# A block-causal attention with a feed-forward layer: the first product by seven block products in seven pieces, the bound of v on ScalarE, and a new order

## The chip, the cores and the metric

The kernel runs on one core of a Trainium2 chip. The metric is the device time of one execution in microseconds (us); less is better. A profile is one execution taken by the hardware profiler. Its engines are named PE (TensorE, matrix products), PEld (TensorE's weight loads), DVE (VectorE), ACT (ScalarE), POOL (GpSimd) and SP (SyncE, which here issues nearly all transfers).

## What is computed

Attention over q, k, v of shape (8 batches, 8 heads, 576 tokens, 64), masked by blocks of 64 tokens, and behind it a layer of two matrix products with h * relu6(h + 3) / 6 between them, on 4608 tokens of width 512 with 2048 inner columns.

```python
scores = np.where(block_i >= block_j, q @ k.T / 8, -1e9)   # per head, blocks of 64
attn = softmax(scores); x = (attn @ v)                      # 4608 x 512 after regrouping
h = x @ w_in                                                # 512 x 2048
g = h * np.clip(h + 3.0, 0.0, 6.0) / 6.0
out = g @ w_out                                             # 2048 x 512
```

## The kernel before

**Precision.** Nearly every product is done on 16-bit halves: an operand is scaled, rounded to a high half, and what is left makes a low half; three products (high by high, high by low, low by high) are summed. The first token piece alone is done in 32 bits. Each matmul fills half of the array's columns (64 weights wide), and two of them, one for each half, stand side by side, so "a row" below is one such half matmul.

**Attention.** 32 slots (8 batches by 4 pairs of heads). For a slot `qk_prep` scales and splits q and k and a transposing DMA turns them, `s_group` makes scores, exponentials and their halves `ph` and `phl`, which transposing DMAs turn into `pT`, and `pv_group` multiplies with v and writes the token piece x. The scale of v is made once for a batch: `v_max` (L958) reduces each slot's tile `vnat` (128 x 640) to its largest magnitude on DVE, POOL takes the maximum over partitions, and the scale and its reciprocal follow.

**The layer.** The tokens are cut into 13 pieces (numbered 0 to 12) of 384 columns, the inner columns into 16 groups of 128 (or 8 pairs c). `ffn1_` (L1682) does an ordinary piece: per group 24 rows of 384 columns into the bank `h`. From piece SW = 7 on, `ffn1_seven` (L1581) takes its place: for each pair c it treats the 256 x 512 by 512 x 384 product as 2 x 2 blocks and does it by seven block products instead of eight (Strassen's scheme in Winograd's form): 84 rows of 192 columns into the banks `u` and `v`, with copies of partial sums (`kept`, or `ph` in the last pieces) and additions between them. Its weights' sums and differences are made once (`w_forms`, L1456) for all c, stored in DRAM (`dr_wf`), and loaded again for each piece and c (`w_get`, L1482): two loads of 256 KB, each into one of NWG = 4 buffers with the tag `wg`. `x_forms` (L1551) makes the sums and differences of the token piece. The second product has the like scheme from piece SG = 11 on; it isn't touched.

**Order.** Nothing is issued directly: a `Recorder` keeps every operation with its operands, and `schedule` (L463) then simulates the engines with a table of costs and takes, on each engine, the ready operation with the lowest key. A key is a planned time plus a number from the table SHIFT, by step (`f1 6 3` is piece 6, group 3 of the first product). All operations are emitted in `emit`, so every row of the profile has the line L673. Buffers with the tag `stage` are slots of one tile that the planner hands out; those with the tag `wg` are a pool's buffers.

Of the kernel before, what the change touches and what calls it, by code (L numbers as in the profile page):

```python
# [67 lines left out]
for _step, _by in (  # L68
# [38 lines left out]
    ("gw", (
        "0:10.7,1:7.9,2:15.4,3:22,4:0.9,6:-2.1,7:11,"
    )),
    ("load_next", (  # L110
        ":-2,"
    )),
    ("maxes", (
        "1:-4.9,2:4.6,3:-7.8,4:-4.4,8:-4.1,"
    )),
# [8 lines left out]
    ("pv_group32", (
        "0 0:0.2,0 1:2,1 0:-3.3,1 1:-2.3,1 2:-0.3,2 0:-3.7,2 1:3.1,2 2:7.1,3 0:-8.5,3 1:-1.3,3 2:15.8,"
    )),
# [1936 lines left out]
```

## Time and profile before

| what | value |
|---|---|
| time, median of 3 runs | 944.58 us (942.45 to 945.48) |
| the profiled execution's own time | 944.98 us |
| its span, first to last instruction | 943.2 us |
| PE, DVE, ACT busy | 99%, 93%, 79% |

The span is 1.78 us shorter than the execution that it was taken from. A busy PE is not yet a PE at its peak, because matmuls are pipelined and overlap in the records; so what a matmul costs is read here from where a run of them starts to where the next one starts. TensorE's granted clock is at the full 2.4 GHz level in every stretch shown below (the column PEclk).

### The profile page before, as it was taken

How to read it: one execution, taken by the hardware profiler on the slowest of the kernel's cores; microseconds unless marked ns; L12 is line 12 of the kernel's file. 1: busy time of each engine (PE TensorE's matmuls, PEld its weight loads, DVE VectorE, ACT ScalarE, POOL GpSimd, SP SyncE). 2: the span in 40 equal slices, each digit the busy share in tenths (PEclk: the TensorE clock that was granted, in tenths of full speed). 3: DMA queues.
4: the chain of work that ended last, by engine and by line, in shares of the span. 5: the costliest groups of instructions: out<-in, count | busy, mean ns of one | idle time of the engine just before them, and what ended most of it. 6: DMA issues, size and time to landing. Idle time of an engine off the chain costs nothing.

```text
span 943.2 us, 33175 instructions
## 1 busy us (share of the span) xinstructions
PE 933.3 (99%) x13478; PEld 704.6 (75%) x13478; DVE 876.6 (93%) x2293; ACT 749.4 (79%) x1995; POOL 43.0 (5%) x146
## 2 busy tenths in 40 slices
PE   8999999999999999999999999999999999999998
PEld 5666446878788776666666677888888888888997
DVE  7999999999889999999999899899898999899975
ACT  6988878888878888878887887888788888576753
POOL 3010100000000000000000000000000000000000
PEclk9999999999999999999999999999999999999999
DMA  7969878899879999988898899899798995442330
GB/s 192 264 215 253 205 137 174 159 185 163 153 158 154 185 166 186 202 159 164 161 192 171 160 221 161 158 208 198 171 210 171 204 199 133 106 124 70 103 92 35
DMA packets 430489, 158.53 MB, mean 168 GB/s; under 512 B 404992, under 2 KB 405504, under 8 KB 430336
## 3 DMA queue, kind: packets, MB, share of 16 engines
q1 hardware_dynamic: 429392, 156.09, 79.9%
q8 instruction: 105, 1.72, 0.8%
q14 instruction: 48, 0.39, 0.2%
q10 hardware_dynamic: 944, 0.33, 0.1%
HBM read 70.25 MB, written 13.63 MB: 89 GB/s over the span
## 4 chain that ended last, share of the span: by engine, by line
PE 87%; DVE 6%; ACT 3%; DMA 2%; issue 1%; POOL 0%; DVEq 0%; ACTq 0%; SPq 0%
PE o L673 36%; PE h L673 20%; PE v L673 9%; PE s L673 7%; PE u L673 6%; PE pv L673 6%; DVE st L673 1%; DVE stages L673 1%; PE sf L673 1%; DMA qkT<-qks 1%; PE pf L673 1%; DMA pT<-ph 1%; PE pt L673 1%; ACT stages L673 1%; DVE win L673 0%
## 5 line engine op out<-in xcount | busy, mean ns | idle before, releaser
L673 PE MATMUL o<-wout,g 128*64 128x512 f16 (+3 forms) x3234 | 409.2, 377 | 0.0
L673 PEld LDWEIGHTS <-g 128*64 128x64 f16 x3174 | 192.0, 110 | 80.6 <-DVE g L673 0.2
L673 PEld LDWEIGHTS <-win 128*64 128x64 f16 x4032 | 207.2, 110 | 46.5 <-issue 2.0
L673 PE MATMUL h<-x,win 128*64 128x384 f16 (+3 forms) x2474 | 220.0, 312 | 0.0
L673 ACT ACTIVATE p<-s,st,esc 128x64 f32<-128x64 f32 (+1 forms) x280 | 163.4, 587 | 12.3 <-DVE phl L673 6.8
L673 DVE TENSOR_REDUCE st<-s 128x1 f32<-128x64 f32 (+1 forms) x280 | 118.9, 444 | 1.9 <-PE s L673 1.6
L673 PEld LDWEIGHTS <-wg 128*64 128x64 f16 x2304 | 105.1, 110 | 8.5 <-issue 1.1
L673 DVE SCALAR_TENSOR_TENSOR g<-stages,g 128x384 f16<-128x384 f32 (+1 forms) x192 | 98.5, 516 | 9.9 <-ACT g L673 9.2
L673 ACT ACTIVATE g<-stages 128x384 f16<-128x384 f32 (+1 forms) x150 | 73.8, 492 | 37.8 <-DVE stages L673 30.0
L673 PE MATMUL s<-qkT 128*64 128x64 f16 (+7 forms) x1120 | 99.8, 287 | 0.0
L673 PEld LDWEIGHTS <-vhl 128*64 128x64 f16 x1680 | 72.8, 110 | 10.9 <-issue 2.4
L673 PEld LDWEIGHTS <-qkT 128*64 128x64 f16 x1120 | 59.3, 110 | 26.2 <-issue 5.8
L673 ACT ACTIVATE stages<-h,eg,sh 128x192 f32<-128x192 f32 (+1 forms) x112 | 62.8, 575 | 16.2 <-PE h L673 15.5
L673 PE MATMUL pv<-pT,vhl 128*64 128x192 f16 (+2 forms) x1680 | 73.8, 233 | 0.4 <-DMA pT<-ph 0.3
L673 PE MATMUL v<-x,wg 128*64 128x192 f16 x1152 | 67.1, 246 | 0.8 <-ACT kept L673 0.8
L673 DVE SCALAR_TENSOR_TENSOR ph<-p,st,ph 128x64 f16<-128x64 f32 (+2 forms) x168 | 67.0, 443 | 0.0
L673 DVE SCALAR_TENSOR_TENSOR phl<-p,st,phl 128x512 f16<-128x512 f32 (+1 forms) x84 | 64.2, 788 | 1.9 <-ACT phl L673 1.6
L673 DVE SCALAR_TENSOR_TENSOR stages<-stages,eg,h 128x384 f32<-128x384 f32 (+1 forms) x96 | 51.5, 538 | 5.7 <-ACT stages L673 5.2
L673 ACT ACTIVATION_READ_ACCUMULATOR p<-s,st,esc 128x1 f32 x280 | 55.3, 197 | 0.0
L673 ACT ACTIVATE ph<-p,st 128x64 f16<-128x64 f32 (+5 forms) x111 | 46.6, 462 | 9.0 <-DVE st L673 8.2
L673 ACT ACTIVATE st<-st,esc 128x1 f32<-128x1 f32 (+2 forms) x130 | 37.2, 290 | 17.1 <-DVE st L673 16.0
L673 ACT ACTIVATE stages<-u,eg,sh 128x384 f32<-128x384 f32 (+1 forms) x64 | 36.0, 588 | 15.1 <-DVE u L673 12.4
(206 smaller groups left out, 1458.9 us busy)
## 6 DMA issues: line engine op xcount, KB each, us to landing
wg<-dr_wf SPq DMA_DIRECT2D x96, 256.0 KB, 3.1
vnat<-in_v_dram SPq DMA_DIRECT2D x64, 128.0 KB, 3.0
qk<-in_q_dram SPq DMA_DIRECT2D x28, 288.0 KB, 3.4
qk<-in_k_dram SPq DMA_DIRECT2D x28, 288.0 KB, 4.1
out_dram<-stages SPq DMA_DIRECT2D x20, 256.0 KB, 3.0
rawi<-in_moe_w_in_dram SPq DMA_DIRECT2D x8, 512.0 KB, 4.4
rawo<-in_moe_w_out_dram SPq DMA_DIRECT2D x8, 512.0 KB, 4.5
dr_wf<-wf SPq DMA_DIRECT2D x16, 256.0 KB, 2.5
```

What stands on the lines that cost most here:

```text
L673: getattr(eng, method)(*map(self.place, args), **{k: self.place(a) for k, a in kw.items()})
```

## The change

Four edits, and with them a new table SHIFT.

1. SW goes from 7 to 6: piece 6 too is done by seven block products. So `pv_group` writes piece 6 as one 32-bit tile, `x_forms` runs for it, `w_get` loads 16 times more, and `w_forms` is planned earlier (WF0 from 4.5 to 3.9, its step from 0.2996 to 0.28).
2. For batches 1 to 7 `v_max` no longer takes the largest magnitude on DVE but the sum of squares on ACT (Square with an accumulator; the squares go to a tile `unread`). The root is taken roughly, by shifting the bits of the sum right by one: one more small DVE operation for a batch.
3. The buffers `wg` become slots of one tile that the planner hands out, as the stages are.
4. Two constants of 128 x 32 and some small tiles move into stage slots or share a tile.

```diff
-VM_ACT = 0
-SW, SA = 7, 11
+SW, SA = 6, 11
-WF0, WFD, WFL = 4.5, 0.2996, 9.7246
+WF0, WFD, WFL = 3.9, 0.28, 9.7246
...
-        "0 0:2,0 1:1.1,0 2:0.3,0 3:16.7,0 4:-1.5,0 5:0.4,0 6:0.1,0 7:-1.8,0 8:0.7,0 9:2.3,0 10:-0.5,"
+        "0 0:21.8,0 1:19,0 2:-10.3,0 3:-61.1,0 4:-94.4,0 5:-75.8,0 6:-46.8,0 7:-8.5,0 8:-1.6,0 9:-39,"
...
-        return str(getattr(a.tensor, "tag", "")).startswith("stage_")
+        return str(getattr(a.tensor, "tag", "")).startswith(("stage_", "wg_"))
...
+            low = 1.0
+            if nm[0] == "v" and nm != "v0":
+                nc.vector.tensor_scalar(pw.bitcast(I32), al.bitcast(I32), 1, None, op0=ALU.logical_shift_right)
+                al, low = pw, 2.0 ** -64
+            nc.vector.tensor_scalar(pw, al, TINY * low, 1.0 / (E_V * low), op0=ALU.max, op1=ALU.mult)
...
+        t, m = vnat[n % NVB], vmax[b][:, hp:hp + 1]
+        if b:
+            nc.scalar.activation(unread, t, AF.Square, accum_out=m)
         else:
-            absmax(vmax[b][:, hp:hp + 1], vnat[n % NVB], AX.XYZ)
+            absmax(m, t, AX.XYZ)
...
-        return attp.tile([P, 2, 2, 2 * P], F16, tag="wg", bufs=NWG, name=f"{nm}{c}_{i}")
+        return drp.tile([P, 2, 2, 2 * P], F16, tag="wg", bufs=NWG, name=f"{nm}{c}_{i}")
```

**ACT in piece 6.** Before, piece 6 asks ACT for `stages<-h6` (the first step of the activation) and the rounding `g6`, among work of the attention (`p`, `st`, `phl`, `ph`) and of the output of piece 5 (`osb5`, `o5`).

```order
L673 ACTIVATE stages_74<-h6_2_1388,eg_584,sh3_1_1217 128x384
L673 ACTIVATE osb5_1392<-o5_0_1258,so5_1391 128x512
L673 ACTIVATE st19_2_1479<-st19_2_1479,esc19_1383 128x2
L673 ACTIVATE g6_2_1390<-stages_74 128x384
L673 ACTIVATE p19_6_1484,st19_2_1479<-s19_2_1_0_1482,st19_2_1479,esc19_1383 128x448
L673 ACTIVATE osb5_1392<-o5_1_1259,so5_1391 128x512
```

After, at the same place:

```order
L676 ACTIVATE kept6_1396<-u6_2_1437 128x192
L676 ACTIVATE p19_7_1505,st19_2_1503<-s19_2_0_0_1504,st19_2_1503,esc19_1410 128x512
L676 ACTIVATE st20_1_1550<-st20_1_1550,esc20_1476 128x1
L676 ACTIVATE stages_74<-u6_2_1437,eg_585,sh3_4_1400 128x384
L676 ACTIVATE g6_4_1440<-stages_74 128x384
L676 ACTIVATE p19_6_1508,st19_2_1503<-s19_2_1_0_1506,st19_2_1503,esc19_1410 128x448
L676 ACTIVATE kept6_1396<-v6_3_1459 128x192
L676 ACTIVATE stages_74<-v6_2_1438,eg_585,sh3_4_1400 128x384
```

The copies `kept6` have come in between, and TensorE's next block product into the same half bank waits for them.

**SP in the middle of piece 6** (`qkT` and `pT` are the transposing DMAs of attention slots 19 to 21, `dr_wf` the stores of the weights' forms). Before:

```order
L673 DMA_TRANSPOSE qkT21_1510<-qks_92 128x27x128
L673 DMA_TRANSPOSE pT19_1_1478<-phl19_6_1486 128x8x128
L673 DMA qk22_1580<-in_q_dram 128x9x64
L673 DMA_TRANSPOSE pT19_1_1478<-phl19_7_1487 128x8x128
L673 DMA dr_wf6_0_1425<-wf6_0_1423 128x1024
L673 DMA qk22_1580<-in_k_dram 128x9x64
L673 DMA_TRANSPOSE pT19_1_1478<-phl19_8_1488 128x10x128
L673 DMA dr_wf6_1_1428<-wf6_1_1426 128x1024
```

After:

```order
L676 DMA wgs_75<-dr_wf3_1_1198 128x1024
L676 DMA wgs_75<-dr_wf6_0_1333 128x1024
L676 DMA_TRANSPOSE qkT21_1536<-qks_93 128x27x128
L676 DMA wgs_75<-dr_wf4_0_1250 128x1024
L676 DMA_TRANSPOSE pT19_1_1502<-phl19_6_1510 128x8x128
L676 DMA wgs_75<-dr_wf4_1_1253 128x1024
L676 DMA_TRANSPOSE pT19_1_1502<-phl19_8_1512 128x10x128
```

The loads of weight forms for piece 6 now stand among the transposes of slots 19 and 20; the stores of the forms that stood there have moved ahead.

**The bound of v for slot 12.** Before, on DVE:

```order
L673 TENSOR_REDUCE vmax3_810<-vnat0_104 128x1
L673 TENSOR_SCALAR st9_0_815<-st9_0_815,esc9_746 128x3
L673 TENSOR_SCALAR g2_4_789<-stages_74 128x384
L673 SCALAR_TENSOR_TENSOR g2_4_789<-stages_74,g2_4_789 128x384
L673 TENSOR_TENSOR st8_2_791<-st8_2_791 128x1
```

After, on ACT:

```order
L676 ACTIVATE ph0_91<-p8_2_763,st8_0_759 128x192
L676 ACTIVATE unread_108,vmax3_811<-vnat0_104 128x640
L676 ACTIVATE p8_3_782,st8_1_780<-s8_1_0_0_781,st8_1_780,esc8_721 128x256
L676 ACTIVATE p8_4_784,st8_1_780<-s8_1_1_0_783,st8_1_780,esc8_721 128x320
L676 ACTIVATE st8_1_780<-st8_1_780,esc8_721 128x1
```

The reduction has left DVE's queue, and one activation of 640 columns stands among ACT's exponentials.

## Rows read from the trace of the kernel before

**Rows 1.** The page: busy time of the engines over the span.

```profile
PE 933.3 (99%) x13478; PEld 704.6 (75%) x13478; DVE 876.6 (93%) x2293; ACT 749.4 (79%) x1995; POOL 43.0 (5%) x146
```

**Rows 2.** Stretches: from:to, length, each engine's busy us (instructions), PEclk, DMA share, GB/s.

```profile
0.00:50.00 50.00, 45.65 (x290) 30.43 (x291) 42.83 (x140) 40.17 (x120) 10.60 (x44) 1.00 0.85 227
...
300.00:540.00 240.00, 240.00 (x3177) 164.22 (x3172) 230.83 (x601) 198.97 (x534) 10.18 (x32) 1.00 0.90 172
540.00:660.00 120.00, 118.39 (x2013) 95.00 (x2009) 112.62 (x296) 98.63 (x277) 3.37 (x14) 1.00 0.98 190
660.00:780.00 120.00, 120.00 (x2089) 99.97 (x2086) 112.35 (x293) 100.73 (x275) 3.10 (x13) 1.00 0.94 190
780.00:940.00 160.00, 159.32 (x2942) 139.69 (x2938) 142.39 (x331) 102.78 (x239) 0.24 (x1) 1.00 0.34 91
...
540.00:570.00 30.00, 29.03 (x496) 21.75 (x491) 27.54 (x76) 23.27 (x63) 1.07 (x3) 1.00 1.09 210
```

**Rows 3.** The chain that ended last: start, us, what, rows in a run.

```profile
240.26 5.85 PE h L673 x72
...
691.29 0.50 PE v L673 x12
691.79 0.99 PE u L673 x24
```

**Rows 4.** Groups by form: line, engine, operation, shapes, count; busy, mean ns.

```profile
L673 PEld LDWEIGHTS <-win 128*64 128x64 f16 x4032 | 207.2, 110 | 46.5 <-issue 2.0 <-DVE stages L673 1.2
...
L673 DVE TENSOR_REDUCE vmax<-vnat 128x1 f32<-128x640 f32 x32 | 25.8, 808 | 0.2
...
L673 ACT ACTIVATE vhl<-vnat,rs_v 128x640 f16<-128x640 f32 x28 | 23.0, 821 | 0.1
...
L673 ACT ACTIVATE kept<-v 128x192 f32<-128x192 f32 x55 | 18.0, 328 | 5.1 <-PE v L673 4.9
L673 DVE TENSOR_TENSOR u<-u,kept 128x384 f32<-128x384 f32 x32 | 17.8, 557 | 6.7 <-PE u L673 5.7 <-ACT st L673 0.8 <-ACT kept L673 0.2
...
L673 DVE TENSOR_TENSOR v<-v,kept 128x192 f32<-128x192 f32 x32 | 11.4, 355 | 0.0
...
L673 ACT ACTIVATION_READ_ACCUMULATOR qks<-qk 128x1 f32 x56 | 10.9, 194 | 0.0
...
L673 DVE SCALAR_TENSOR_TENSOR x<-pv,x 128x192 f16<-128x192 f32 x20 | 6.6, 348 | 0.0
...
L673 DVE TENSOR_TENSOR stages<-x 128x384 f32<-128x384 f32 x12 | 6.5, 546 | 0.0
...
L673 DVE TENSOR_TENSOR xr<-x,xr 128x768 f16<-128x768 f32 x6 | 5.7, 944 | 0.0
```

**Rows 5.** Timeline at 559 to 571 us: start, us, what [idle before, releaser].

```profile
559.90 0.68 ACT L673 ACTIVATE qks<-qk 128x576 bf16<-128x576 f32 x1 [1.35 <-DMA qkT<-qks]
...
561.94 0.69 PE L673 MATMUL v<-xr,win 128*64 128x192 f16 x12 [0.40 <-DVE stages L673]
...
569.11 0.83 ACT L673 ACTIVATE phl<-p,st 128x640 f16<-128x640 f32 x1 [1.37 <-issue]
...
570.21 0.69 PE L673 MATMUL v<-x,wg 128*64 128x192 f16 x12 [0.78 <-ACT kept L673]
```

**Rows 6.** Tile wg: what its readers waited for, and its loads' time to landing.

```profile
  issue: 1.1, 1
...
DMA to landing us min/median/max: 2.5/3.1/5.4
```

**Rows 7.** SP's timeline at 764 us: a transpose and the weight load behind it.

```profile
764.09 5.15 SPq L673 DMA_TRANSPOSE qkT<-qks  x1
769.33 0.53 SPq L673 DMA_DIRECT2D wg<-dr_wf  x1
```

**Rows 8.** PE's timeline in the first microseconds, and at the end.

```profile
7.17 1.04 PE L673 MATMUL sf<-qkf 128*128 128x128 f32 x6 [1.17 <-DVE qkf L673]
...
932.77 6.67 PE L673 MATMUL o<-wout,g 128*64 128x512 f16 x60
```

More of the change, by code (lines that the diff above doesn't have):

```diff
@@ L69 @@
     ("f1", (
[16 rows of a table removed]
[16 rows of a table added]
     )),
     ("f2", (
[18 rows of a table removed]
[20 rows of a table added]
     )),
     ("gw", (
[L108 removed]
+        "0:3.6,1:-10.2,2:-30.3,3:-20,4:-44.3,5:14.4,6:0.6,7:7.3,"
     )),
     ("load_next", (
[L111 removed]
+        ":2.5,"
     )),
     ("maxes", (
[L114 removed]
+        "1:-8.6,2:4.9,3:25.7,4:2,8:2.7,"
     )),
     ("pv_group", (
[6 rows of a table removed]
[6 rows of a table added]
     )),
     ("pv_group32", (
[L125 removed]
+        "0 0:10.9,0 1:2.6,0 2:-8.8,1 0:-16.4,1 1:-0.5,1 2:32.4,2 0:-3,2 1:14.5,2 2:6.8,3 0:-3.4,"
@@ L126 @@
+        "3 1:-20.8,3 2:21.9,"
     )),
     ("qk_load", (
-        "4:-16.6,5:14.5,6:20,7:53.9,8:3,9:-7,10:30.3,11:26.4,12:1.6,13:45.8,14:4.6,15:-6.8,16:-6.6,"
-        "17:-3.2,18:3.5,19:-3.4,20:-12.4,21:-0.7,22:1.4,23:6.5,24:14.4,25:-20.6,26:2,27:0.4,28:63.8,"
-        "29:-15.9,30:-2.9,31:-0.5,"
+        "4:27.1,5:-5.4,6:-12.7,7:4.1,8:-12.6,9:28.2,10:-12.3,11:3.6,12:-14.3,13:29.5,14:9.8,15:9.3,"
+        "16:4.7,17:-6.5,18:-6.8,19:-36,20:-22.1,21:-32.7,22:-22.9,23:-1.3,24:0.8,25:23.4,26:42.9,"
@@ L131 @@
+        "27:-44.9,28:-22.3,29:-14.7,30:0.1,31:-5.8,"
     )),
     ("qk_load32", (
-        "0:-0.7,1:-9.7,2:-3,3:0.8,"
+        "0:-30.8,1:-39.5,2:-7,3:-1.8,"
     )),
     ("qk_load32_rest", (
-        "0:-1.9,1:-8.1,2:10.7,3:0.1,"
+        "0:-0.5,1:1.7,2:-15.1,3:4.3,"
     )),
     ("qk_prep", (
-        "4:0.2,5:-11.3,6:-10.5,7:0.7,8:-2.7,9:1.3,10:1,11:1.6,12:-4.7,14:2.8,15:2.4,16:5.5,17:-0.8,"
-        "18:13.3,19:18,20:17.7,21:0.8,22:-7.6,23:2.5,24:-4.7,25:-2.9,26:-0.5,27:-0.4,28:1,29:1.4,30:-1.1,"
@@ L141 @@
-        "31:-2,"
+        "4:-0.5,5:69.8,6:-32.1,7:3.1,8:5.7,9:7.7,10:-48,11:-0.4,12:8.7,13:-3.5,14:-8.7,15:-14.8,16:-16.3,"
+        "17:5.5,18:23.1,19:4.6,20:50.9,21:13.9,22:0.6,23:-43.3,24:-3.6,25:31.3,26:-10,27:-16.4,28:-32.3,"
+        "29:29,30:3.9,31:0.4,"
     )),
     ("qk_prep32", (
-        "0 0:5.8,0 1:-3.5,1 0:-6,1 1:7.1,2 0:35.5,2 1:1.1,3 0:-3.1,3 1:-0.3,"
+        "0 0:-13.2,0 1:55.8,1 0:1.5,1 1:7.9,2 0:52,2 1:-13.6,3 0:20.5,3 1:72.2,"
     )),
     ("s_block32", (
[4 rows of a table removed]
[4 rows of a table added]
     )),
     ("s_group", (
[9 rows of a table removed]
[9 rows of a table added]
@@ L179 @@
+        "13:5.8,14:-8.9,15:30.1,16:-25.9,17:29.4,18:-4.5,19:-10.9,20:10.6,21:-21.2,22:-26.8,23:-15.6,"
+        "24:-95,25:63.8,26:-62.1,27:30.1,28:-17.3,29:18.3,30:7.2,31:23.6,"
     )),
     ("v_max", (
-        "0:-21.7,1:-14.2,2:-19.1,3:3.3,4:3,5:-2.5,6:-0.9,7:-2.9,8:-3,9:4.9,10:19.5,11:2.3,12:5.7,13:22,"
-        "14:-11.9,15:-4,16:-5.5,17:-5.9,18:-1.7,19:5.7,20:-1.3,21:2.6,22:-8.6,23:13.6,24:-8.4,25:0.2,"
-        "26:-7.3,27:5.3,28:9.5,29:-15.8,30:-9.6,31:1.2,"
+        "0:-6.6,1:59.8,2:-7.1,3:-31.2,4:-25.3,5:3.2,6:-0.7,7:-1.5,8:-1.9,9:32,10:-14,11:11.3,12:-14.9,"
@@ L184 @@
+        "13:10.9,15:11.6,16:19.8,17:8.2,18:21,19:6.2,20:44.3,21:14,22:7.6,23:56.8,24:-10.3,25:-4.3,"
+        "26:-23.3,27:-103.6,28:3,29:-11.6,31:17.2,"
     )),
     ("v_prep", (
-        "4:2.5,5:9.7,6:3.4,7:17,8:-0.3,9:19.8,10:-19.7,11:-4.7,12:1.2,13:-1,14:-2.9,15:2.7,16:0.3,17:9,"
-        "18:-1.6,19:12.4,20:5,21:-0.1,22:1.7,23:0.7,24:-14.9,25:-0.4,26:-5.2,27:-10.8,28:-14.3,29:-3.7,"
-        "30:1.5,31:8,"
+        "4:-6.2,5:27.6,6:4.6,7:-10.5,8:-0.8,9:-4,10:-35.3,11:-0.8,12:5.5,13:43.4,14:3.9,15:10.6,16:24.2,"
@@ L189 @@
+        "17:-0.7,18:-5.6,19:-10.6,20:1.8,22:3.6,23:3.7,24:-39.8,25:86.6,26:-2.6,27:2.7,28:-4.5,29:25,"
+        "30:-11.6,"
     )),
     ("wf", (
-        "0:-3.6,1:-1,2:-0.6,3:3.7,4:-3.3,5:9.3,6:1.9,7:6.2,"
+        "0:33.2,1:-5.6,2:1.4,3:8.6,5:6.2,6:7.2,7:12.3,"
     )),
     ("wg", (
[5 rows of a table removed]
[6 rows of a table added]
     )),
     ("xf", (
-        "7:-3,8:1,9:0.8,10:-1.3,11:10,12:-2.1,"
+        "6:2.6,7:-28.2,8:1.6,9:33.7,10:-6.7,11:-3.4,12:22.2,"
     )),
@@ L665, in schedule @@
         self.span = max(o.end for o in ops)
-        self.slot = {x: f[1] for x, f in got.items() if self.meta[x][0].startswith("stage_")}
+        self.slot = {x: f[1] for x, f in got.items() if self.meta[x][0].startswith(("stage_", "wg_"))}
         return sorted(ops, key=lambda o: (o.start, o.n))
@@ L678, in place @@
             return a
-        base = self.stages if a.dtype == F32 else self.stages.bitcast(a.dtype)
+        base, slots = self.rings[str(a.tensor.tag).split("_")[0]]
+        base = base if a.dtype == F32 else base.bitcast(a.dtype)
         (pitch, n), *dims = a.ap
@@ L682, in place @@
         row = base.ap[0][0]
-        return bass.AP(base.tensor, p0 * row + self.slot[a.tensor.name] * (row // self.NST) + f0, [(row, n), *dims])
+        return bass.AP(base.tensor, p0 * row + self.slot[a.tensor.name] * (row // slots) + f0, [(row, n), *dims])
 @with_exitstack
@@ L720 @@
     T0 = TP
-    nc.NST = NST_B
     NTA, NTR = 3, 2
@@ L741 @@
     drp = ctx.enter_context(tc.tile_pool(name="dr", bufs=1, space=bass.MemoryType.DRAM))
-    nc.stages = wpool.tile([P, NST_B * DM], F32, tag="stages", name="stages")
+    nc.rings = {x: (wpool.tile([P, n * DM], F32, tag=x + "s", name=x + "s"), n) for x, n in (("stage", NST_B), ("wg", NWG))}
     ps_s = ctx.enter_context(tc.tile_pool(name="ps_s", bufs=3, space=bass.MemoryType.PSUM))
@@ L799 @@
     ident = wpool.tile([P, P], F32, tag="ident", name="ident")
-    ramp = wpool.tile([P, 32], F32, tag="ramp", name="ramp")
-    rows = wpool.tile([P, 32], F32, tag="rows", name="rows")
+    ramp, rows = (drp.tile([P, 32], F32, tag="stage", bufs=4, name=x) for x in ("ramp", "rows"))
     nc.gpsimd.memset(ident, 0.0)
@@ L817 @@
         nc.gpsimd.memset(halves[h * BLK:(h + 1) * BLK, h * BLK:(h + 1) * BLK], 1.0)
-    one = wpool.tile([P, 1], F32, tag="one", name="one")
+    few = wpool.tile([P, 2], F32, tag="few", name="few")
+    one, three = few[:, :1], few[:, 1:]
     nc.gpsimd.memset(one, 1.0)
-    three = wpool.tile([P, 1], F32, tag="three", name="three")
     nc.gpsimd.memset(three, 3.0)
@@ L939 @@
         nc.gpsimd.memset(t[BLK:, NJ - 1], 0.0)
+    unread = wpool.tile([P, NJ, 2, D], BF16, tag="unread", name="unread")
     vscale = {}
@@ L959, in v_max @@
         b, hp = divmod(n, NPAIR)
-        if n < VM_ACT:
-            ab = attp.tile([P, S], F32, tag="p", bufs=NPB, name=f"va{n}").bitcast(BF16)
-            ab = ab[:, :NJ * 2 * D].rearrange("p (j h d) -> p j h d", h=2, d=D)
-            nc.scalar.activation(ab, vnat[n % NVB], AF.Abs, accum_out=vmax[b][:, hp:hp + 1])
+        t, m = vnat[n % NVB], vmax[b][:, hp:hp + 1]
+        if b:
+            nc.scalar.activation(unread, t, AF.Square, accum_out=m)
         else:
-            absmax(vmax[b][:, hp:hp + 1], vnat[n % NVB], AX.XYZ)
+            absmax(m, t, AX.XYZ)
         if hp == NPAIR - 1:
@@ L1086, in qk_prep32 @@
                 ]
-                parts = [parts[0][:, :S], parts[1], attp.tile([P, 4 * P], F32, tag="wg", bufs=NWG, name=f"qkf{n}_2")]
+                parts = [parts[0][:, :S], parts[1], drp.tile([P, 4 * P], F32, tag="wg", bufs=NWG, name=f"qkf{n}_2")]
             qkT[n] = parts[0], []
@@ L1157, in s_block32 @@
         if i % 2:
-            pr = attp.tile([P, 4 * P], F32, tag="wg", bufs=NWG, name=f"pf{n}_{i}")
+            pr = drp.tile([P, 4 * P], F32, tag="wg", bufs=NWG, name=f"pf{n}_{i}")
         else:
@@ L1670, in ffn1_f32 @@
             )
-        r = attp.tile([P, T0], F32, tag="wg", bufs=NWG, name=f"r0_{f}")
+        r = drp.tile([P, T0], F32, tag="wg", bufs=NWG, name=f"r0_{f}")
         nc.scalar.activation(r, ps, AF.Relu, bias=three, scale=1.0)
```

9 lines of the change are left out of this document (3 added, 6 removed), and 125 rows, old and new, of the table SHIFT.

## The prediction, as put on record

> **What bounds the kernel now.** I began with the page's engine totals: PE is busy for 99% of the span, DVE for 93%, ACT for 79% [rows 1]. A busy PE may still hide waits, so next come the stretches [rows 2]. PE misses 4.35 us of the first 50 us (50 less 45.65), none at all of the 240 us from 300 to 540, 1.61 us from 540 to 660, none from 660 to 780 and 0.68 us of the last 160. Over those stretches that is 6.6 us of idleness, so nearly all of the time is PE at work. The third view is the chain that ended last, to see whether the work itself runs at its pace: 72 rows of `h` take 5.85 us from start to start, 81.25 ns each, and 24 rows of `u` take 0.99 us, 41.25 ns each [rows 3]. Half as many columns take half the time, plus next to nothing. So in mid-kernel the price of an edit is the number of rows that it takes from PE or gives it, and everything else counts only where it makes PE wait.
>
> **The change part by part.**
>
> *Piece 6 by seven products.* Removed: 16 groups of 24 rows of 384 columns, 384 rows by 81.25 ns = 31.20 us. Added: 8 pairs c of 84 rows of 192 columns, 672 rows by 41.25 ns = 27.72 us. Both stand on PE, which waits for nothing in the stretch where piece 6 lies now, so the difference is on the path: **-3.48 us**. No other matmul changes in number.
>
> The Trainium skill, in "TensorE: Matmul & The Clock Gate", section "LDWEIGHTS (loading the stationary operand)", speaks against this: it prices a weight load by its columns divided by 1.2 in ns, 53 ns for 64 columns. If the loads of two rows side by side had to be done one after the other and set the pace, a pair would need 107 ns, an estimate by which the 336 new pairs would cost 35.9 us and the sum would be +4.7 us. The runs of 41.25 ns a row, load included, don't show that pace [rows 3].
>
> *What piece 6 then asks of DVE and ACT.* DVE gets 8 additions into `u` (557 ns), 8 into `v` (355), and in `x_forms` 8 operations of 384 columns (546), one of 768 (944) and one more of 546; it loses 8 lower halves of x (348) [rows 4]: 4.46 + 2.84 + 4.37 + 1.49 - 2.78 = +10.4 us. The 24 copies `kept` at 328 ns are 7.9 us on ACT or DVE, and the six roundings of `x_forms`, priced as their subtractions, 3.7 us. None of it is on PE; what hides it is the free time of the two engines. From 300 to 540 they are busy for 230.83 + 198.97 of 480 us [rows 2], so 50 us are free, and the 22 us asked for fit, the more as `w_forms`, whose operations stay the same in number, moves ahead of piece 6. If that cover were gone, PE would wait for a copy or for a rounded `g`, by about 0.4 to 0.8 us at a time, as it does at 561.94 and 570.21 [rows 5].
>
> *The bound of v on ACT.* DVE loses 28 reductions of 808 ns, 22.6 us. ACT gets 28 activations of 640 columns. A Square with an accumulator isn't in the trace; the nearest rows are the scaling of the same tile, 821 ns, and the reading of an accumulator, 194 ns [rows 4]. So 1.0 us each, 28.4 us in all, at the least 0.8 and at the most 1.1 us. Behind each stand exponentials and copies on ACT's queue, as the order shows, and a late `kept` can reach PE. It is one such delay for each attention slot, and ACT is free for 4.8 to 5.1 us in 30 (240 - 198.97 = 41 in 240, 120 - 100.73 = 19.3 in 120) [rows 2]. Cost: nothing on PE, down to -0.5 us (DVE earlier) and up to +1 us. The small shift for each batch is seven DVE operations, far off the path.
>
> *Loads and the queue of SP.* 16 more loads of 256 KB stand among the transposes. From 300 to 540 the DMA share is 0.90, with the loads from 540 to 660 it is 0.98, and 1.09 in its first 30 us [rows 2]. In those 30 us PE loses 0.97 us, and its two waits trace back to ACT waiting for a transpose that was late: 1.35 us for `qkT`, and 1.37 us in front of a `phl` whose buffer a transpose still read (the profile names no engine, so this is an inference) [rows 5]. From 660 to 780 the same loads run at 0.94 and PE loses nothing. Piece 6 takes some 75 us of the kernel. At the pace of 540 to 660 that is 1.0 us, at the pace of 660 to 780 it is 0. I take the middle: **+0.5 us**, and keep 0 and 1.0.
>
> *The slots of `wg` and the new order.* How long a weight load may take is given by the work on PE between the last reader of its slot and its first reader. Counted in rows, that work is under 9 us for 33 of 92 loads before and for 61 of 108 now; the shortest is 5.5 us before and 5.9 now. A load lands after 3.1 us, 5.4 at worst [rows 6], and a `qkT` transpose ahead of it can hold SP for 5.15 us [rows 7]. Before, all the short ones together cost PE one wait of 1.1 us that may be theirs [rows 6]. I take 0 and keep +1. The start and the end have no reason to change by much: 4.35 us of waiting in the first 50 us, the first of it for the copies of the first transposed q and k, which stand in the same order as before [rows 8]; behind them scores, exponentials and transposes of the first slots stand in another order, and that may give or take 2 us. At the end the same 60 rows of `o` close the program [rows 8]. Taken: 0.
>
> **The sum.** -3.48 + 0.5 = **-3.0 us**. The profiled execution took 944.98 us, so 942.0; it lies 0.4 us over the median of the runs, so the median becomes **941.6 us**. Its own bounds: -3.48 to -3.48 + 1.0 + 1.0, with -0.5 for DVE: 940.6 to 943.1, about 940.3 to 943.2 with the runs' scatter.
>
> **The rivals.**
>
> *The new order also takes out waits.* For it: PE idles 1.61 us from 540 to 660 and 4.35 us at the start, and a new order moves both. Against: the start is a chain of dependent steps. If the first goes and a quarter of the second (1.1 us): 944.58 - 3.48 - 2.7 = 938.4 us.
>
> *The start gets longer.* If its waits grow by half (2.2 us): 944.58 - 3.0 + 2.2 = 943.8; if they double, 945.9.
>
> *The transposes come late all through pieces 6 to 10: slower.* Place: ACT waits for `qkT` or `pT`, and behind it on its queue stand the copies `kept` that PE needs. For it: just that happened at 560 and 570, DVE and ACT together get 28 us more work (-22.6 + 28.4 + 22), and the room for loads is smaller. Against: 660 to 780 is free of it at the same load. Price: 0.97 us for each 30 us, as in the stretch from 540 to 570, over the 11 such stretches from 450 to 780 is 10.7 us, less the 1.6 that are there now, so 944.58 - 3.48 + 9.1 = 950.2 us. It decides the sign where it passes 3.48 us, and the bound of slower below from 6.3 us, 0.7 us for each 30.
>
> *The weight loads don't hide.* 288 rows more bring 288 more loads of 110 ns [rows 4]; if all were exposed, 31.7 us, and if one in four, 7.9 us: 944.58 - 3.48 + 7.9 = 949.0. The pace in rows 3 speaks against it.
>
> **How the numbers follow.** The runs lie within 0.3%, and a difference under 0.3% (2.8 us: 941.75 to 947.4) can't be told from none. The forecast 0.42, of which a little over half (0.24) is under 941.75. The order takes out waits: 0.23, all faster. The start longer: 0.13 (0.10 same, 0.03 slower). Late transposes: 0.20 (0.07 same, 0.13 slower). Exposed loads: 0.02, slower. So faster 0.47, same 0.35, slower 0.18. The range goes from 937.5, which leaves out the best fifth of the second case, to 949.0, which leaves out the worse half of late transposes: 0.15 in all.
>
> **What would show it.** The row counts of `u`, `v` and `h`, and a run of `u` rows at 41.25 ns also where piece 6 lies. PE's idleness in 30 us steps from 450 to 540: under 1 us in all if I am right, 1 us in each if the transposes come late, with ACT waiting for DMA `qkT` or with "issue" in front of `phl`. PE busy in the first 50 us beside 45.65. DVE's total lower by some 10 us and ACT's higher by 30 to 40 if the copies go to ACT. I am wrong in the main if piece 6 runs at 41 ns and the time still doesn't fall; then the order has turned the gain into waits elsewhere, and the stretches will show where.

## The result, and the profile after

| | median, us | lowest to highest | runs |
|---|---|---|---|
| before | 943.77 | 942.45 to 945.48 | 6 |
| after | 951.81 | 949.08 to 952.01 | 6 |
| forecast | 941.6 | range 937.5 to 949.0 | |

The changed kernel takes 1.0076 times as long (95%: 1.006 to 1.0093): slower by 8.0 us, where 3.0 us less were forecast. Its profiled execution took 949.68 us, with a span of 947.9 us. It is one of the two shorter of the six, and the profiled execution of the kernel before (944.98 us) lies above its median: so the two traces are 4.7 us apart where the medians are 8.0.

The page of the kernel after, totals of the engines (compare [rows 1]):

```profile
PE 933.3 (98%) x13764; PEld 713.2 (75%) x13764; DVE 877.1 (93%) x2324; ACT 767.9 (81%) x2051; POOL 41.9 (4%) x144
```

Its stretches, in the columns of [rows 2]:

```profile
0.00:50.00 50.00, 46.03 (x292) 30.77 (x293) 43.83 (x142) 40.36 (x124) 10.48 (x42) 1.00 0.84 221
50.00:300.00 250.00, 247.14 (x2933) 172.97 (x2933) 230.40 (x637) 211.21 (x552) 14.84 (x42) 1.00 0.92 181
300.00:540.00 240.00, 239.58 (x3474) 179.14 (x3472) 232.40 (x612) 203.85 (x558) 8.78 (x31) 1.00 0.95 184
450.00:540.00 90.00, 90.00 (x1476) 72.75 (x1473) 84.61 (x222) 76.32 (x207) 3.16 (x12) 1.00 1.02 200
540.00:660.00 120.00, 120.00 (x2083) 95.80 (x2080) 114.71 (x309) 105.63 (x292) 3.06 (x13) 1.00 1.07 197
660.00:780.00 120.00, 117.44 (x1992) 91.47 (x1987) 110.02 (x289) 103.35 (x288) 4.56 (x15) 1.00 0.97 190
780.00:940.00 160.00, 159.17 (x2978) 140.81 (x2976) 143.87 (x339) 102.99 (x240) 0.15 (x1) 1.00 0.37 94
```

The products of piece 6 lie between about 463 and 532 us, and there PE waits for nothing. The loss is elsewhere. PE idles 2.86 us from 50 to 300, where it idled 0.10 before, and 2.56 us from 660 to 780, where it idled not at all. The 1.61 us from 540 to 660 are gone, and the start is no longer than it was (3.97 us for 4.35).

The span grew by 4.7 us although PE has 3.5 us less to do, so 8.2 us of waiting were added. The idleness in the stretches shows 3.9 of it (10.64 less 6.74 us): a matmul's recorded duration stretches over part of a wait. Measured from start to start against the pace of each kind of row, behind the first 60 us, the excess is 3.5 us before and 11.9 after, and it sits at some twenty places: mainly 126, 171 to 201, 225, 300, 420, 684 to 711 and 727 to 783 us.

What the engines waited for there is seen best at the tile `phl`. Before, its writers waited once for a transposing DMA that still read the buffer, and twice with no releaser named, as at 569.11 [rows 5] (releaser, us in total, times):

```profile
  issue: 1.9, 2
...
  DMA pT<-phl: 0.6, 1
```

After, nine times for the DMA:

```profile
  DMA pT<-phl: 6.6, 9
```

One of the nine, in the timeline of the kernel after:

```profile
219.95 1.41 DVE L676 SCALAR_TENSOR_TENSOR phl<-p,st,phl 128x512 f16<-128x512 f32 x2
...
222.07 2.68 SPq L676 DMA_TRANSPOSE pT<-phl  x2
...
227.06 0.83 ACT L676 ACTIVATE phl<-p,st 128x640 f16<-128x640 f32 x1 [1.75 <-DMA pT<-phl]
...
227.79 0.47 ACT L676 ACTIVATE x<-pv 128x384 f16<-128x384 f32 x1
227.92 0.88 DVE L676 SCALAR_TENSOR_TENSOR phl<-p,st,phl 128x640 f16<-128x640 f32 x1 [1.70 <-ACT phl L676]
...
228.72 0.55 DVE L676 SCALAR_TENSOR_TENSOR x<-pv,x 128x384 f16<-128x384 f32 x1
...
229.33 0.46 PE L676 MATMUL s<-qkT 128*64 128x320 f16 x4 [1.49 <-DVE x L676]
```

A slot has three `phl` tiles and the pool has two buffers for them. At 222.07 SP issues the transposes of the first two; ACT must write the third into the first's buffer and waits 1.75 us until that transpose has read it. Behind this instruction on ACT's queue stands the copy `x<-pv`, behind it on DVE's the second half of that copy, and PE's next matmul waits for that: 1.49 us. In the kernel before, the same place goes without a wait, though its third tile follows its transposes by only 4.2 us:

```profile
219.12 2.74 SPq L673 DMA_TRANSPOSE pT<-phl  x2
...
223.35 0.82 ACT L673 ACTIVATE phl<-p,st 128x640 f16<-128x640 f32 x1
```

The transposes also land later than before. From 150 to 300 us the median from issue to landing of those into `pT` is 4.4 us, and it was 3.8, though the traffic is nearly the same (171 GB/s for 169). Why they land later isn't shown.

### The profile page after: what moved, and what is told of

Read it like the earlier page. It is cut to its first block, busy times and chain, and to the rows that moved or that the text cites. A ratio compares the mean times of both kernels' runs of the same rounds, so it can differ in the third digit from the quotient of the medians.

```text
span 947.9 us, 33891 instructions
## 1 busy us (share of the span) xinstructions
PE 933.3 (98%) x13764; PEld 713.2 (75%) x13764; DVE 877.1 (93%) x2324; ACT 767.9 (81%) x2051; POOL 41.9 (4%) x144
## 4 chain that ended last, share of the span: by engine, by line
PE 71%; DVE 14%; ACT 6%; DMA 5%; issue 2%; SPq 1%; POOL 0%; ACTq 0%; DVEq 0%
PE o L676 30%; PE h L676 12%; PE v L676 10%; PE u L676 7%; PE s L676 5%; PE pv L676 5%; DMA pT<-phl 3%; DVE st L676 2%; DVE phl L676 2%; DVE stages L676 2%; ACT p L676 2%; DVE ph L676 2%; ACT stages L676 2%; DVE g L676 1%; DVE wout L676 1%
## 5 line engine op out<-in xcount | busy, mean ns | idle before, releaser
L676 PE MATMUL h<-x,win 128*64 128x384 f16 (+3 forms) x2098 | 186.7, 311 | 0.2
L676 ACT ACTIVATE p<-s,st,esc 128x384 f32<-128x384 f32 (+2 forms) x280 | 163.1, 587 | 14.3 <-DVE phl L676 6.5
L676 PEld LDWEIGHTS <-wgs 128*64 128x64 f16 x2688 | 122.5, 110 | 11.6 <-issue 1.0
L676 DVE TENSOR_REDUCE st<-s 128x1 f32<-128x384 f32 (+6 forms) x280 | 119.1, 446 | 2.0 <-PE s L676 1.7
L676 PE MATMUL s<-qkT 128*64 128x512 f16 (+7 forms) x1120 | 102.2, 287 | 4.1 <-ACT p L676 2.5
L676 PE MATMUL v<-x,wgs 128*64 128x192 f16 x1344 | 77.9, 246 | 0.5 <-ACT kept L676 0.5
L676 DVE SCALAR_TENSOR_TENSOR ph<-p,st,ph 128x64 f16<-128x64 f32 (+3 forms) x168 | 67.8, 445 | 0.6 <-ACT ph L676 0.5
L676 ACT ACTIVATE stages<-h,eg,sh 128x192 f32<-128x192 f32 (+1 forms) x96 | 52.4, 560 | 9.8 <-PE h L676 7.2
L676 ACT ACTIVATE ph<-p,st 128x256 f16<-128x256 f32 (+5 forms) x116 | 48.7, 462 | 6.9 <-DVE st L676 5.8
L676 ACT ACTIVATE stages<-v,eg,sh 128x384 f32<-128x384 f32 (+1 forms) x72 | 41.8, 596 | 8.4 <-PE v L676 4.3
```

Source lines behind the costliest of these rows:

```text
L676: getattr(eng, method)(*map(self.place, args), **{k: self.place(a) for k, a in kw.items()})
```

## The experiments

Four theories: **V**, the bound of v costs ACT more than was allowed; **T**, the added weight loads crowd the transposes; **O**, the new order itself has the waits in it; and **B**, formed after the first runs, that late transposes act through the two buffers of `phl`. A new table of times would give a wholly different order, so all runs keep the order of their kernel (but for those that move instructions on purpose) and change an operation where it is emitted. Differences below are to the median of the kernel before in the same batch, that is, of the runs made together (943.17 to 944.11 us), by which the kernel after stands at +8.0 us.

### The bound of v

**e1_v_on_dve**, the kernel after:

```diff
+if method == "activation" and args[2] == AF.Square:
+    self.nc.vector.tensor_reduce(
+        self.place(kw["accum_out"]), args[1], axis=AX.XYZ, op=ALU.max, apply_absolute_value=True
+    )
+    continue
```

> The changed kernel with its order held, instruction by instruction; only the bound of v for batches 1 to 7 is again a largest magnitude on DVE (28 reductions at the places where the 28 activations stood). The changed kernel takes 951.8 us, the kernel before 943.8. Theory V (the bound on ACT holds up ACT): the 8 us come back for the larger part, 946 us or less. Theory T (weight loads crowd the transposes): no change beyond the one wait that the trace shows behind an activation `unread` (ACT waits 1.24 us for vnat at 300 us, PE loses 0.9 us there), so 950.5 to 952. Theory O (the waits are in the new order itself): the same 950.5 to 952, or a little more, since DVE gets 22.6 us of work that the order has no room made for.

Measured: 964.75 us, +21.6.

**e3_v_on_act**, the kernel before:

```diff
+if method == "tensor_reduce" and args[0].tensor.name[:4] == "vmax" and args[0].tensor.name != "vmax0":
+    self.nc.scalar.activation(self.nc.unread, args[1], AF.Square, accum_out=args[0])
+    continue
```

> The kernel before with its order held; only the bound of v for batches 1 to 7 is made as in the change, 28 Squares with an accumulator on ACT at the places of the 28 reductions, and one small DVE shift for a batch. Theory V: slower by most of the 8 us, 948 us or more. Theories T and O: 28 activations of about 0.92 us fit where ACT was free, 943 to 946 us.

Measured: 953.36 us, +10.2. Of this, about 2 us are lost at the start: the condition didn't catch batch 0, whose bound the kernel after leaves on DVE (32 Squares in the trace, not 28). So at a held order the work has no room on either engine that wasn't planned for it. Neither number is the price of the edit itself; for that the work was shortened where it stands.

**e5_short_square**, the kernel after, and **e8_before_short_max**, the kernel before:

```diff
+if method == "activation" and args[2] == AF.Square:
+    args = (args[0][:, :1, :1], args[1][:, :1, :1], AF.Square)
```

```diff
+if method == "tensor_reduce" and args[0].tensor.name[:4] == "vmax":
+    args = args[0], args[1][:, :1, :1]
```

> The changed kernel with its order held; only the 28 Squares on ACT read 64 of their 640 columns, so v is scaled by a bound from a tenth of the numbers. That takes some 0.65 us from each, 18 us from ACT. Theory V (the bound of v on ACT is what makes the changed kernel late): the larger part of the 8 us comes back, 946 us or less. Theory T (weight loads crowd the transposes): only the stall of 0.9 us at 300 us may go, 950.5 to 952. Theory O (the new order leaves too little between a result and its reader, on all engines): ACT is less often late, 949.5 to 951.

> The kernel before with its order held; only the 32 reductions for the bound of v on DVE read 64 of 640 columns, which takes some 0.7 us from each, 22 us from DVE: the gain that the change can have from DVE at most. Theory V and T: DVE's free time is cover enough, 943 to 944 us. Theory O: a little of the 3.5 us of stalls goes, 941.5 to 943 us.

Measured: 950.00 us, +5.9, so 2.1 us less than the kernel after; and 942.18 us, -1.9, with DVE busy for 860.9 us where it was 876.6. These edits shorten the work and don't remove it: a Square with its accumulator from 0.92 to 0.44 us, a reduction from 0.81 to 0.21. What they took away was worth about as much on ACT as on DVE, so moving the bound shows no gain. The 0.92 us of a whole Square are near the 1.0 that was taken:

```profile
L676 ACT ACTIVATE unread<-vnat x28: 719/727/762, 74.2 to 705.2; 128x640 bf16<-128x640 f32 x28
L676 ACT ACTIVATION_READ_ACCUMULATOR unread<-vnat x28: 185/192/226, 74.8 to 705.8; 128x1 f32 x28
```

(Tile `unread` of the kernel after: count, least, median and greatest ns, first and last start.) What was missed is that ACT's time isn't free.

### The weight loads

**e2_half_loads**:

```diff
+if method == "dma_start" and str(getattr(args[0].tensor, "tag", "")) == "wg" and args[0].dtype == F16:
+    args = args[0][:, :512], args[1][:, :512]
```

> The changed kernel with its order held; only each of the 112 loads of weight forms brings 128 KB in place of 256 KB (the first 512 of 1024 columns), so the other half of those operands holds older numbers and the output is not the reference's. PE does the same matmuls. Theory T (weight loads crowd the transposes): the stalls that end in a late transfer go, 1.6 us at 225, 0.9 at 300, 2.2 from 699 to 711 and perhaps 1.2 at 783 to 813 us, so 946 to 947 us. Theory V: 951 to 952. Theory O: only a part of these goes, 949 to 951, since the order leaves some readers too close behind their transfer even at light traffic, and the stalls at 126, 684, 735 and 759 us have no transfer at their end.

Measured: 952.03 us, but the edit had no effect: the tiles don't carry that tag at this point, and the loads in its trace still have 256 KB. It stands as a second measurement of the kernel after, +8.9, and shows that figures from single batches are good to about 1 us. Its trace is of an execution of 951.91 us, and there a `phl` that waited only 0.33 us in the trace of the kernel after (at 295.57 us) waits 2.69 us and holds PE up for 2.15:

```profile
296.93 0.72 ACT L678 ACTIVATE phl<-p,st 128x512 f16<-128x512 f32 x1 [2.69 <-DMA pT<-phl]
...
299.16 0.52 PE L678 MATMUL s<-qkT 128*64 128x384 f16 x4 [2.15 <-ACT p L678]
```

So in one and the same kernel it differs between executions which of these places costs time.

**e6_half_loads**, the kernel after, and **e7_before_half_loads**, the same edit in the kernel before:

```diff
+if method == "dma_start" and args[0].tensor.name[:2] == "wg" and args[0].dtype == F16:
+    args = args[0][:, :512], args[1][:, :512]
+if method == "matmul" and args[1].tensor.name[:2] == "wg" and args[1].dtype == F16:
+    w = args[1]
+    args = args[0], bass.AP(w.tensor, w.offset - w.offset % 1024 + w.offset % 512, w.ap), args[2]
```

> The changed kernel with its order held; each of the 112 loads of weight forms brings 128 KB in place of 256 KB, and the matmuls take all their weights from the half that was loaded, so the output is not the reference's. (In the earlier run e2_half_loads the edit did not reach the loads: they still brought 256 KB, so that run is a second measurement of the changed kernel, 952.0 us.) Theory T: the stalls that end in a late transfer go, 946 to 947.5 us. Theory V: 951 to 952. Theory O: 949 to 951, since the transposes are late by their own order and by each other.

> The kernel before with its order held and the same edit: its 96 loads of weight forms bring 128 KB each. Theory T: the stalls around 560 and 570 us go, 942 to 942.5 us. Theories V and O: 942.5 to 944 us; what this edit gives here is to be taken from what it gives to the changed kernel.

Measured: 947.57 us, +3.5, and 942.72 us, -1.4. Half the bytes give 4.6 us in the kernel after and 1.4 in the kernel before: the kernel after, with 112 such loads for 96, depends more on the transfers' pace. **e10_both_short** has the edits of e5 and e6 together:

> The changed kernel with its order held and two edits at once: Squares over 64 columns (alone -1.8 us, 950.0) and weight loads of 128 KB (alone -4.2 us, 947.6). The output is not the reference's, since half of the weight forms is left out. If V and T are separate parts of the loss they add up, 945 to 946.5 us, and the 4 us that then remain over the forecast of 941.6 are the order's. If they relieve the same stalls, 947 to 948 us.

Measured: 948.48 us, +4.8, no better than the half loads alone.

**e14_no_loads_for_6**, the kernel after without the 16 loads that piece 6 added (its products read `win` instead), and **e16_before_no_loads_for_7**, its counterpart for the first such piece of the kernel before:

```diff
+if method == "dma_start" and args[0].tensor.name[:4] == "wg6_":
+    continue
+if method == "matmul" and args[1].tensor.name[:4] == "wg6_":
+    args = args[0], self.nc.win[:, 0, 0, 0, :64], args[2]
```

> The changed kernel with its order held; the 16 weight loads that piece 6 adds are left out, and the matmuls of piece 6 that used them take weights from the tile `win` (so piece 6 is not the reference's). PE, DVE and ACT do the same work; SP issues 16 transfers less. Theory T, by count: the traffic is that of the kernel before, and of the 2.8 us that halving all loads gave here more than in the kernel before, most comes back: 948 to 949.5 us. If only the loads of the last pieces, behind which the larger stalls stand (684 to 814 us), matter: 951 to 952, since piece 6 (450 to 525 us) shows no stall. My prediction had +0.5 us for these loads: 951.3.

> The kernel before with its order held and without the 16 weight loads of its first piece by seven products, piece 7 (the same edit; its numbers are not the reference's): the control for e14_no_loads_for_6. Its stalls at 560 and 570 us stand right there, so 942 to 943.5 us; what it gives is to be taken from what e14_no_loads_for_6 gives.

Measured: 950.46 us, +6.6, so 1.4 us less than the kernel after; and 943.84 us, no difference. So the 16 added loads explain little of the 11 us between forecast and result. And none of the loads from `dr_wf` is issued before 316 us in the kernel after, so PE's 2.86 us of idleness from 50 to 300 can't come from them. The late transposes stay in e14, one of them at 297 us:

```profile
291.05 3.57 SPq L680 DMA_TRANSPOSE pT<-phl  x2
...
297.43 0.72 ACT L680 ACTIVATE phl<-p,st 128x512 f16<-128x512 f32 x1 [2.88 <-DMA pT<-phl]
...
299.67 0.52 PE L680 MATMUL s<-qkT 128*64 128x384 f16 x4 [2.34 <-ACT p L680]
```

**e4_more_loads** sent the loads of piece 7 twice, in the kernel before:

```diff
+if method == "dma_start" and args[0].tensor.name[:4] == "wg7_":
+    self.nc.sync.dma_start(*args)
```

> The kernel before with its order held; only the 16 loads of weight forms for piece 7 are issued twice, right behind each other into the same buffer: 16 loads of 256 KB more, as many as the change adds, where the traffic is densest (540 to 600 us). Theory T: the stalls of that stretch, 1.6 us, double or triple, 946 to 949 us. Theories V and O: SP and the DMA engines have the room, 943.5 to 945.5 us.

Measured: 979.66 us, +36.5, which says nothing on traffic: the second load writes the same buffer, so SP's queue waits for the first to land (47.6 us in 19 times, where it was 2.3 us in 3), and everything behind it is late. The waits on PE (us in total, times, longest):

```profile
PEld L675 <- DMA wg<-dr_wf: 17.4, 8, 3.7
...
PE u L675 <- DMA wg<-dr_wf: 11.1, 7, 3.1
```

### The order

**e9_six_moves** puts six instructions of the kernel after behind others, so that what PE waits for no longer stands behind a `phl` that is held:

```diff
+MOVES = ((1664, 1687), (1665, 1664), (2937, 2271), (1023, 943), (5524, 5386), (5441, 5336))
+plan = self.schedule()
+for n, behind in MOVES:
+    o = next(x for x in plan if x.n == n)
+    plan.remove(o)
+    plan.insert([x.n for x in plan].index(behind) + 1, o)
```

> The changed kernel with six of its instructions moved a little later on their own engine, and nothing else: at 126 us DVE's `am_w` (it waited 1.40 us for POOL) behind the small `st` that stood behind it; at 227 us the two halves of a `phl` (ACT waited 1.75 us for a transposing DMA to leave the buffer) behind the two halves of `x` that stood behind them; at 300 us the activation `unread` (1.24 us for its load) behind four exponentials and copies; at 708 us the sum over k (ACT 1.40 us for its load) behind a copy `kept`, and a `phl` (DVE 1.69 us for a transposing DMA) behind a `g`. Theory O (what stands in a row is the cause, not the amount of work or traffic): the stalls of PE at these places, 1.3 + 1.6 + 0.6 + 1.6 us, go for the most part, and 947 to 949 us come out. Theories T and V: the transfers are as late as before, PE only waits for the next instruction, 950.5 to 952 us.

Measured: 951.70 us, +8.0, no change. At the place shown above PE now waits for the transpose itself:

```profile
227.73 0.85 PE L684 MATMUL pv<-pT,vhl 128*64 128x192 f16 x18 [1.01 <-DMA pT<-ph]
```

**e11_after_reordered** and **e12_before_reordered** emit the whole program in another order, given as a list of instruction numbers.

> The changed kernel with all its instructions on the engines that the plan gave them, but some of them moved by a few places in their queues (some 410 of 2324 on DVE, 250 of 1633 on ACT, 150 of 2510 groups of matmuls, 105 of 549 on SP), so that a reader stands farther behind what it waits for where transfers come late. Theory O: the forecast of the change comes out, 939 to 944 us. Theory T: at most the half, 945 to 949 us, since the loads still crowd the transposes. Theory V: the same 946 to 951 us.

> The kernel before, with its instructions moved in the same manner (some 460 on DVE, 270 on ACT, 180 groups of matmuls, 117 on SP). It stands beside e11_after_reordered: two kernels with orders of the same making, so their difference is that of the work. Theory O: 3.5 us of stalls from 60 us on can go at most, 940 to 943 us, and e11_after_reordered is 1 to 3 us below it. Theories T and V: e11_after_reordered stays above it by 3 us or more.

Measured: 965.99 us, +22.3, and 944.82 us, +1.2. The first is 11.7 us late at its first `phl` transpose (146.5 us for 134.8), by some 3.6 us at its start and by one wait of 9.5 us for GpSimd (below), and its `phl` still waited at 241 us; it doesn't tell O from B.

### GpSimd

The timeline of POOL in the kernel after:

```profile
119.64 1.77 POOL L676 TENSOR_SCALAR qks<-qks 128x576 f16<-128x576 f16 x1 [7.02 <-ACT ph L676]
121.42 0.46 POOL L676 MEMSET ph<- 128x256 f16 x2
127.73 0.37 POOL L676 PARTITION_ALL_REDUCE al_w<-wm  x1 [5.85 <-ACT p L676]
...
128.13 0.17 DVE L676 TENSOR_SCALAR am_w<-al_w 128x2 f32<-128x2 f32 x1 [1.40 <-POOL al_w L676]
```

The plan gave POOL one scaling of `qks`. The operand of the reduction behind it was ready at 124.4 us, but the reduction started at 127.73: between a tensor operation and a partition reduction the trace has a record that reconfigures POOL, at 122.1 us, 5.6 us ahead of the reduction. The Trainium skill, in "GPSIMD Engine Reference", section "2.1 Instruction dispatch", gives approximately 6 us for the first call to a freshly loaded routine; the 5.6 us here agree, though this reduction had run before, at 111.94 us. **e13_pool_free** does this one scaling on ACT:

```diff
+if o.eng == "gpsimd" and method == "tensor_scalar" and args[0].tensor.name[:3] == "qks":
+    self.nc.scalar.activation(*map(self.place, args[:2]), AF.Copy, scale=args[2])
+    continue
```

> The changed kernel with its order held; only one instruction changes its engine: the single TENSOR_SCALAR that the new plan gives to POOL (`qks`, at 119.6 us) goes to ACT, where 20 others like it run. In the trace of the changed kernel POOL sets its configuration anew behind it (MODIFY_POOL_CONFIG at 122.1 us), and its next reduction over partitions, `al_w`, starts only 5.6 us later, at 127.73, 3.4 us after its operand was there; DVE waits 1.40 us for it and PE loses 1.3 us. The kernel before has no such instruction on POOL and no second setting. Theory O (one misplaced instruction of the plan is a part of the loss): the stall at 126 us goes, -1 to -1.5 us, 950.3 to 951. If `al_w` is late for another reason: no change, 951.8.

Measured: 950.32 us, +6.5, so 1.5 us less than the kernel after, which is within the error of a single batch. The reduction now starts 2.7 us sooner, and DVE doesn't wait for it:

```profile
125.03 0.36 POOL L679 PARTITION_ALL_REDUCE al_w<-wm  x1 [2.67 <-ACT stages L679]
...
127.08 0.16 DVE L679 TENSOR_SCALAR am_w<-al_w 128x2 f32<-128x2 f32 x1
```

### The sum, and a third buffer

Each of the three reliefs (e5, e13, e14) is within the scatter of the kernel after. **e15_three_reliefs** has all three:

> The changed kernel with its order held and three edits at once: POOL's one instruction on ACT, no loads for piece 6 (its numbers are not the reference's), Squares over 64 columns. What remains above 941.6 us is what the new order itself leaves PE to wait for, without the new work on ACT, the added traffic and POOL. If these three are the cause, 944 to 946 us; if the order is, 948 to 950 us.

Measured: 947.42 us, +3.6 (ratio 1.0045, 1.0029 to 1.0062). Together they are worth 4.4 us; added singly, 5.1. By the ratios to the kernel before it is 2.9 us (1.0045 for 1.0076), and the two intervals just touch, so the size of this sum is not well known.

**e17_third_buffer** is e5 with a third buffer for `phl`: from slot 6 on, the first of a slot's three tiles gets a place of its own (the room comes from the shortened Squares' output, and the tile holds `ident`, `halves` and `ident2` in the first part of the program). **e18_four_reliefs** is e15 with the same buffer.

```diff
+def third(name):
+    x = name.split("_")
+    return x[0][:3] == "phl" and int(x[0][3:]) > 5 and x[1] == "6"
...
+        if isinstance(a, bass.AP) and third(a.tensor.name):
+            e = self.nc.extra
+            (pitch, n), *dims = a.ap
+            p0, f0 = divmod(a.offset, pitch)
+            return bass.AP(e.tensor, p0 * e.ap[0][0] + f0, [(e.ap[0][0], n), *dims])
```

> The changed kernel with its order held, with Squares over 64 columns as in e5_short_square (950.0 us; the space that their output leaves is needed here), and with a third buffer for `phl`: from slot 6 on the first of a slot's three `phl` tiles has a buffer of its own, so the third tile need not wait until the transposing DMA of the first has left its buffer. In the trace of the changed kernel ACT waits 3.4 us in all and DVE 3.2 us in front of a `phl` for that DMA, and in e14_no_loads_for_6 ACT waited 2.88 us at 297 us, with what PE needs queued behind it. Theory B (late transposes, through this buffer): those stalls go, 946 to 948.5 us. Theory O (PE's waits are spread over all kinds of readers): one wait takes the place of the other, 949 to 950.5 us.

> As e15_three_reliefs (947.4 us: POOL's one instruction on ACT, no loads for piece 6, Squares over 64 columns; the numbers of piece 6 are not the reference's), and with the third buffer for `phl`. Theory B: 943 to 945.5 us, so nearly all of the loss over the forecast of 941.6 has a name. Theory O: 946.5 to 948 us; the rest is then the order's own waits.

Measured: 944.71 us, +1.2 (ratio 1.0013, 1.0001 to 1.0025), 4.7 us less than e5's +5.9 (ratio 1.0067, 1.0046 to 1.0087); and 942.54 us, -1.0 (ratio 0.9989, 0.998 to 0.9997), 4.6 us less than e15. Twice the same gain, from intervals that don't overlap, and in the traces of e5 and e17 every engine has the same instructions in the same order. In e5 the writers of `phl` waited 12 times for the DMA, 7.2 us in all, in e17 once, 0.3 us. What the writers of `phl` waited for in e15:

```profile
  DMA pT<-phl: 9.0, 11
```

and in e18:

```profile
  DMA pT<-phl: 0.2, 1
```

On the third buffer itself, the tile `extra`, its writers waited for no DMA (all their waits from 150 to 900 us):

```profile
  DVE st L690: 1.8, 5
  issue: 0.6, 2
```

The transposes land no sooner: from 150 to 300 us their median from issue to landing is 4.4 us in the kernel after and in e17. So it is the buffers that hold ACT and DVE up, not a shortage of bandwidth by itself; B holds for this part. How much of the same 4.6 us the half loads of e6 relieve wasn't tried. The page of e18:

```profile
PE 929.9 (99%) x13764; PEld 709.2 (75%) x13764; DVE 876.3 (93%) x2324; ACT 756.4 (80%) x2052; POOL 41.5 (4%) x143
```

The gap between forecast (-3.0) and result (+8.0) is 11.0 us:

| part | us | from |
|---|---|---|
| two buffers of `phl` | 4.6 | e15 to e18 |
| Squares, GpSimd's scaling, loads of piece 6 | 4.4 | after to e15; singly 2.1, 1.5, 1.4 |
| not assigned | 2.0 | e18 to the forecast |

By the ratios the three parts are 5.3, 2.9 and 2.0 us, so the split is good to about 1.5 us. The forecast had 0.5 us for loads that e18 leaves out, which puts 2.5 us among what isn't assigned; the Squares, shortened to half in e18, may hold some of it.

By the pages, PE stands idle for 10.2 us of the span in e18 and for 9.9 in the kernel before, and the spans differ by 3.1 us (940.1 for 943.2), about the forecast. But this execution of e18 (941.85 us) is 0.7 under its median, and that of the kernel before 1.2 over its own, so these traces don't place what isn't assigned. What idleness e18 has behind the start lies mainly from 660 to 780, 1.64 us (the kernel before had 1.61 from 540 to 660). The greatest waits on PE's timeline there:

```profile
682.73 0.62 PE L690 MATMUL s<-qkT 128*64 128x512 f16 x4 [0.67 <-ACT p L690]
...
703.83 0.44 PE L690 MATMUL v<-x,wgs 128*64 128x192 f16 x6 [0.32 <-ACT kept L690]
```

Around the first no transfer is waited for, which speaks for the order itself (O); ahead of the second ACT waited 1.27 us for a load of k. No run took these apart. A third buffer in the kernel before wasn't tried, nor the kernel after with whole Squares, a third buffer and the scaling off GpSimd, which needs room that the whole Squares' output takes. No run beat the kernel before with the whole computation.

## Why the prediction was wrong, step by step

**Piece 6, -3.48 us: right.** The chain of the kernel after shows a run of 24 rows of `u` in piece 6 at the pace of [rows 3]:

```profile
463.83 0.99 PE u L676 x24
```

The number of rows rose by 286 (13478 to 13764 [rows 1]) where 288 were forecast, and PE waits for nothing there. PE's busy time is 929.9 us in e18, where most waits are gone, 3.4 less than before. So the weight loads hide. The rule of the Trainium skill ("TensorE: Matmul & The Clock Gate", section "LDWEIGHTS (loading the stationary operand)") that was set against this, by which 64 columns take an estimated 53 ns, doesn't set the pace of rows that take 41 ns with their loads.

**What DVE and ACT are asked for, at nothing: right for piece 6, wrong as a rule.** PE waits for no `kept` and no rounding in piece 6. But DVE was to lose some 10 us and ACT to gain 30 to 40; measured, +0.5 and +18.5. By the groups of rows, the reductions took 22.5 us off DVE as forecast, and by difference the order gave it some 13 us of other work, mostly copies and roundings that ACT did before.

**The bound of v, nothing, with -0.5 to +1: wrong.** Half of the Squares' time was worth 2.1 us on ACT, and DVE's relief, worth 1.9 us in the kernel before, was filled up again. The step that failed in this term is "ACT is free for 4.8 to 5.1 us in 30". That is an average. ACT takes its instructions in order (at 226.06 us the products for `x<-pv` were done, and ACT stood idle until 227.06, because the held `phl` was first on its queue), so its idle time lies where it waits; an instruction of 0.9 us put ahead of a copy delays the copy, however much idle time follows.

**The loads, +0.5 with 0 to 1: perhaps too small.** 1.4 us by e14, within the error of a single batch.

**The slots and the new order, 0 with up to +1: the step that failed.** The slots of `wg` were counted through, and no PE wait on them is in the trace. The same count, how much work lies between a buffer's last reader and its next writer, wasn't made for `phl`, though the row for it was at hand: 1.37 us in front of a `phl` whose buffer a transpose still read [rows 5]. It was taken for a mark of the stretch from 540 to 570 and its loads. In fact it belongs to a ring of two buffers for three tiles, in every slot, and the order, together with how late the transposes land in it, decides how often it bites: at most three times before, nine times after. GpSimd's scaling isn't in the prediction at all; one instruction on an engine that is busy for 4% cost some 1.5 us by e13, and in the traces PE's 0.91 us of idleness at 129.98 us is gone in e13, e15 and e18.

**The start: right**, 46.03 us busy of 50 for 45.65.

**The rivals.** "The transposes come late" named the mechanism: ACT waits for `pT`, and what PE needs stands behind it on the queue. It gave 950.2 us, 1.6 under the result, and that nearness is in part luck, for its place was wrong. It was priced over pieces 6 to 10, from 450 to 780 us, at the pace of 540 to 570; in the trace, 540 to 660 is now free of waits, and 2.86 us of idleness lie from 50 to 300, where no new loads stand. It had 0.20, and the forecast 0.42. The range of the forecast ended at 943.2 because an unknown order was bounded by +1 us with no row behind the bound but one of `wg` [rows 6]. The row had a price for one such wait, 0.78 us on PE [rows 5]; once in each of 28 slots would have been 22 us as an upper end, and the nine times that it happened are 7 by it, 4.6 as measured.

## What to carry to other kernels

The free share of an in-order engine covers nothing by itself: for each instruction that is added or moved, ask what stands behind it on its queue and who waits for that. When the order changes, go through every ring of buffers that a DMA reads from, and count the work between its reader and its next writer, because there a late transfer becomes a wait. Look for the lone instruction that a planner put on another engine; the one on GpSimd cost some 1.5 us here.
